# Grouping the value products of an attention stage, and the order of work around them

## The chip, the cores and the metric

The kernel runs on one core of one Trainium2 chip. TensorE (PE; its weight loads are listed apart as PEld) multiplies, VectorE (DVE), ScalarE (ACT) and GpSimd (POOL) work elementwise, SyncE (SP) issues most DMAs. Each engine takes its own queue in program order and waits on semaphores of the others. The metric is the device time of one execution in microseconds (us).

## The reference

```python
q_rot, k_rot = (rotate(q), rotate(k))            # 4 batches, 8 heads, 576 tokens, 64 per head
scores = scale * np.matmul(q_rot, k_rot.transpose(0, 1, 3, 2))
scores = scores - np.max(scores, axis=-1, keepdims=True)
attn = np.exp(scores)
attn = attn / (np.sum(attn, axis=-1, keepdims=True) + 1e-09)
x = np.matmul(attn, v)                           # to (2304, 512)
x = moe(x)                                       # RMS norm, gate and value (512 -> 1536), silu, out
return moe2(x)                                   # 8 experts, one per token
```

All three parts run in one launch. The change lies in the first, attention.

## The kernel before, in words

The 32 heads are taken as 16 pairs. The method `attention` is a loop over steps g; five steps are a head, ten a pair. `plan` is a table of actions with an offset each: an action of head i falls on step 5 i + offset, one of a pair p on step 10 p + offset, and within a step the actions are issued in the table's order, which is the order in every engine's queue. The actions that matter here:

- `ropeA`, `ropeC`, `ropeH`, `ropeL` rotate q and k of a pair (GpSimd's products, VectorE's sum, ScalarE's copy of the high part, VectorE's low part).
- `TQ` transposes a head's q and k with ten TensorE products into two PSUM tiles `t1` and `t2`; `TE` copies them out on ScalarE (first q, then k).
- `SM` makes the scores of one fifth of the queries (`s`), whose maximum over the keys VectorE takes (L288); `MT` transposes the five maxima of a head (L296), and a DMA carries them into a row of `qB`.
- `ST` makes the scores with keys on partitions (`sT`, four products, L312 and L314), and ScalarE takes their exponential into `E` (L315). `s`, `sT` and `t1` share three PSUM buffers in turn (`psA`), so each waits until the third one before it has been emptied.
- `AV` (L327) multiplies `E` with the values `vraw`: half u of the queries is a sum over five blocks j of keys, for the two heads of the pair in the left and right 64 columns of the array. It issues one block, two products, per step. The last block has 64 keys; both heads' share one tile, in the upper and lower 64 rows. `UE` copies the result out on ScalarE, scaled and squared.
- `EP` (GpSimd) and `ED` (VectorE) add four blocks of `E`; `DN` makes from them the denominators and `SQ` the sums of squares, with 32-column tiles, into a PSUM tile of a single buffer (`psC`, shared with `t2` and the transposed maxima); `stat` adds them up on VectorE at once.
- After every fourth pair, `W0` and `W` take reciprocals and roots of these sums and scale the batch's rows on VectorE, in pieces that `wstep` issues, two a step. From g = 70 on, `conv_step` converts weights of the next part, one piece in ten steps, on step 9 of each (`gr=(9,)`).

Behind attention stand the gated part (up to some 850 us) and the experts; the change touches no line of theirs.

## Time and profile before

| | us |
|---|---|
| median of 3 runs | 1163.78 |
| lowest, highest | 1163.47, 1176.99 |
| span of the profiled execution | 1164.5 |
| TensorE busy | 1071.4 (92%) |
| VectorE busy | 746.5 (64%) |
| ScalarE busy | 462.8 (40%) |
| GpSimd busy | 351.3 (30%) |

The profile is of one execution; its span runs from the first to the last instruction. Busy times are sums over a span with stages of very different limits, so a change in attention has to be read from the rows of that stage. The ends of TensorE's products are modelled and overlap the next start; intervals between starts are what the engine really takes. A granted clock of 1.00 is TensorE's 2.4 GHz, 0.50 is 1.2 GHz.

### The profile page before, as it was taken

The page shows a single profiled execution, that of the slowest core. Times are in us where ns is not written, and L with a number is a line of the kernel's source. Part 1 is how long each engine was busy: PE and PEld are TensorE (multiplying, and loading weights), DVE is VectorE, ACT ScalarE, POOL GpSimd, SP SyncE. Part 2 cuts the span into 40 slices and gives each one's busy share as a digit, 9 for nine tenths or more (in the row PEclk, how much of TensorE's full clock was granted, in tenths as well). Part 3 has the DMA queues.
Part 4 walks back from the last instruction along what each step waited for, and adds up shares of the span by engine and source line. Part 5 has one row for each costly group of instructions (what it writes and reads, how often), then busy time and mean ns, then how long its engine had stood idle before and what let it go on. Part 6 is the DMA issues. An engine that isn't in the chain of part 4 may idle for free. (4 is left out here: it accounts for less than half of the span.)

```text
span 1164.5 us, 17859 instructions
## 1 busy us (share of the span) xinstructions
PE 1071.4 (92%) x6406; PEld 873.1 (75%) x6406; DVE 746.5 (64%) x1415; ACT 462.8 (40%) x992; POOL 351.3 (30%) x374
## 2 busy tenths in 40 slices
PE   4999999999998899999999999999998979999595
PEld 3756656655565589899999999998877858988383
DVE  7587878889875856556565555562477645654263
ACT  3555555555556432422222222222345434533152
POOL 7547657657725501112011110110011211311211
PEclk9889989999999999999999999999999999999798
DMA  4333353343231201111122111101065655653464
GB/s 128 77 78 88 82 139 101 95 113 106 75 92 42 86 19 47 55 40 55 34 97 68 46 37 46 46 10 55 29 229 163 207 162 174 217 181 118 141 217 120
DMA packets 75990, 113.97 MB, mean 98 GB/s; under 512 B 18537, under 2 KB 43393, under 8 KB 75843
## 3 DMA queue, kind: packets, MB, share of 16 engines
q1 hardware_dynamic: 72162, 100.25, 29.8%
q0 software_dynamic: 3680, 11.91, 3.0%
q8 instruction: 74, 1.21, 0.5%
q14 instruction: 74, 0.60, 0.2%
HBM read 85.91 MB, written 12.17 MB: 84 GB/s over the span
## 5 line engine op out<-in xcount | busy, mean ns | idle before, releaser
L733 PE MATMUL gv<-xh,whi 128*128 128x384 f32 x576 | 197.0, 342 | 0.9 <-ACT xh L711 0.9
L733 PE MATMUL gv<-xl,whi 128*128 128x384 f32 x576 | 194.7, 338 | 0.5 <-DVE xl L715 0.5
L733 PE MATMUL gv<-xh,wlo 128*128 128x384 f32 x576 | 194.6, 338 | 0.0
L315 ACT ACTIVATE E<-sT 128x576 f32<-128x576 f32 (+1 forms) x160 | 104.0, 650 | 142.8 <-PE sT L314 142.8
L288 DVE TENSOR_REDUCE m<-s 128x1 fp32r<-128x576 f32 (+1 forms) x160 | 119.1, 749 | 61.2 <-PE s L287 58.5
L647 POOL TENSOR_TENSOR wlo<-cvt,whi 128x256 fp32r<-128x256 f32 x66 | 50.9, 774 | 334.0 <-ACT whi L646 333.9
L743 DVE TENSOR_TENSOR s<-s,gv 128x384 f32<-128x384 f32 x72 | 39.7, 553 | 154.3 <-PE gv L733 147.0
L327 PE MATMUL av<-E,vraw 128*64 128x288 f32 (+1 forms) x640 | 116.5, 444 | 1.5 <-ACT sq L338 1.3
L733 PEld LDWEIGHTS gv<-xh,whi 128*128 128x128 f32 x576 | 108.9, 189 | 6.4 <-issue 3.4
L733 PEld LDWEIGHTS gv<-xl,whi 128*128 128x128 f32 x576 | 109.1, 189 | 2.3 <-DVE xl L715 0.8
L742 ACT ACTIVATE s<-gv 128x384 f32<-128x384 f32 x72 | 34.9, 492 | 187.3 <-PE gv L733 187.3
L733 PEld LDWEIGHTS gv<-xh,wlo 128*128 128x128 f32 x576 | 108.9, 189 | 0.0
L312 PEld LDWEIGHTS sT<-qT,kT 128*128 128x128 f32 (+1 forms) x320 | 47.2, 187 | 67.5 <-issue 31.9
L761 PE MATMUL yps<-whi,hh 128*128 128x512 f32 x216 | 87.6, 406 | 6.4 <-ACT yacc L766 5.4
L312 PE MATMUL sT<-qT,kT 128*128 128x288 f32 (+1 forms) x320 | 86.4, 353 | 5.4 <-DVE m L288 2.4
L776 DVE TENSOR_TENSOR yacc<-yacc,yps 128x512 f32<-128x512 f32 x99 | 67.8, 686 | 32.3 <-PE yps L761 30.9
L345 POOL TENSOR_TENSOR e<-E 128x576 f32<-128x576 f32 x32 | 48.5, 1517 | 126.3 <-DVE es L349 117.7
L761 PE MATMUL yps<-wlo,hh 128*128 128x512 f32 x216 | 85.6, 396 | 0.0
L761 PE MATMUL yps<-whi,hl 128*128 128x512 f32 x216 | 85.6, 396 | 0.0
L287 PE MATMUL s<-kT,qT 128*128 128x288 f32 (+1 forms) x320 | 78.5, 333 | 3.5 <-DVE m L288 2.4
L1266 POOL DMA_INDIRECT x<-ysc,ix x27 | 32.9, 1219 | 152.9 <-DVE vi L1103 76.5
L1373 POOL DMA_INDIRECT out<-cvt,ix x20 | 23.5, 1176 | 166.7 <-DVE cvt L1371 114.2
(285 smaller groups left out, 2131.9 us busy)
## 6 DMA issues: line engine op xcount, KB each, us to landing
raw<-in_w SPq DMA_DIRECT2D x52, 512.0 KB
stt<-in_w SPq DMA_DIRECT2D x26, 512.0 KB
stt<-in_w_gate SPq DMA_DIRECT2D x24, 256.0 KB
stt<-in_w_val SPq DMA_DIRECT2D x24, 256.0 KB
stt<-in_w_out SPq DMA_DIRECT2D x24, 256.0 KB
qB<-qT SPq DMA_DIRECT2D x32, 144.0 KB
kB<-kT SPq DMA_DIRECT2D x32, 144.0 KB
qT<-qT SPq DMA_DIRECT2D x32, 144.0 KB
```

What stands on the lines that cost most here:

```text
L287: nc.tensor.matmul(s[:n, u, 0:288], qA[:, j * 128:j * 128 + n], kA[:, u * 288:u * 288 + 288], start=True, stop=True)
L288: nc.vector.tensor_reduce(m[:n, j:j + 1], s[:n, :, 0:288], axis=AX.XY, op=ALU.max)
L312: nc.tensor.matmul(s[:n, u, 0:288], kA[:, j * 128:j * 128 + n], qA[:, u * 288:u * 288 + 288], start=True, stop=False)
L315: nc.scalar.activation(e.rearrange("p (u c) -> p u c", u=2), s[:n, :, 0:288], AF.Exp, scale=0.125)
L327: self.nc.tensor.matmul(av[64 * h:64 * h + 64, 0:288], V[r, x, j * 64:j * 64 + 64], E[r, x, j, 288 * u:288 * u + 288], start=(j == 0), sto ...
L345: self.nc.gpsimd.tensor_tensor(t, E[:, h, 2 * k, :], E[:, h, 2 * k + 1, :], op=ALU.add)
L647: nc.gpsimd.tensor_tensor(lo, f, fr(hi), op=ALU.subtract)
L733: nc.tensor.matmul(t[:, :CH], w[:, k], r[:, k], start=(n == 0), stop=(n == 11))
L742: nc.scalar.activation(s, ps[0][:, :CH], AF.Silu)
L743: nc.vector.tensor_tensor(s, s, ps[1][:, :CH], op=ALU.mult)
L761: nc.tensor.matmul(ps, l, r[:, 2], start=(n == 0), stop=(n == tot - 1))
L776: nc.vector.tensor_tensor(old[:, t], old[:, t], ps, op=ALU.add)
```

## The change

Value products: `AV` issues all five blocks of a half at one step (ten products), at steps 13 and 18 of a pair where blocks stood at steps 10 to 19; `DN` stays at 18 and `SQ` goes from 21 to 23, each behind a group. From step 160 on, in the tail, blocks are issued singly as before. The last block takes all 128 rows: the values of the two heads lie in tiles of their own whose other half is zeros. `TQ` transposes 128 rows in the fifth block, too. `ED` goes from step 11 to 8, the rotations of q and k are issued apart, the low parts and rotations of VectorE go to other steps (`early` keeps the first two pairs), `stat` is issued at the end of the next step, `wstep` issues four pieces on the step of a value group and one on three others, and the conversion goes from step 9 to step 3.

```diff
     plan = (
-        ("UE1", 20), ("UE0", 15), ("ST", 0), ("MT", -3), ("TQ", -10), ("SM", -8), ("AV", 10), ("TEq", -10), ("LV", 3),
-        ("SQ", 21), ("ropeHq", -14), ("ropeHk", -14), ("QD", -4), ("TEk", -10), ("ropeLq", -13), ("DN", 18),
-        ("EP0", 5), ("ropeA", -21), ("ropeLk", -13), ("ED", 11), ("LQ", -13), ("ropeCk", -15), ("ropeCq", -16),
-        ("EP1", 5),
+        ("UE1", 20), ("UE0", 15), ("ST", 0), ("MT", -3), ("TQ", -10), ("SM", -8), ("AV", 13), ("TEq", -10), ("LV", 3),
+        ("SQ", 23), ("ropeHq", -14), ("ropeHk", -14), ("QD", -4), ("TEk", -10), ("ropeLq", -13), ("DN", 18),
+        ("ropeAq", -21), ("EP0", 5), ("EP1", 5), ("ropeAk", -20), ("ropeLk", -12), ("ED", 8), ("LQ", -13), ("ropeCk", -15),
+        ("ropeCq", -17),
     )
+    early = {"ropeLk": -13, "ropeCq": -16, "ropeAk": -21}
...
         for i in range(2):
-            self.raw["v", i] = sm.tile([P, 2, 320], F32, name=f"vraw{i}")
+            t = self.raw["v", i] = sm.tile([P, 2, 320], F32, name=f"vraw{i}")
+            nc.gpsimd.memset(t[64:128, 0, 256:320], 0.0)
+            nc.gpsimd.memset(t[0:64, 1, 256:320], 0.0)
...
-                    self.nc.sync.dma_start(t[64 * h:64 * h + 64, 0, 256:320], s2[h, 512:576, :])
+                    self.nc.sync.dma_start(t[64 * h:64 * h + 64, h, 256:320], s2[h, 512:576, :])
...
-            for j in range(4):
-                nc.tensor.transpose(t1[:, x, j * 128:j * 128 + 128], src[:, h * 5 + j].rearrange("p e d -> p (e d)"), self.idr)
-            nc.tensor.transpose(t2[:, x * 64:x * 64 + 64], src[:64, h * 5 + 4].rearrange("p e d -> p (e d)"), self.idr[:64, :64])
+            for j in range(5):
+                o = t1[:, x, j * 128:j * 128 + 128] if j < 4 else t2[:, x * 128:x * 128 + 128]
+                nc.tensor.transpose(o, src[:, h * 5 + j].rearrange("p e d -> p (e d)"), self.idr)
...
         for h in range(2):
-            r, x = (slice(0, n), h) if j < 4 else (slice(64 * h, 64 * h + 64), 0)
-            self.nc.tensor.matmul(av[64 * h:64 * h + 64, 0:288], V[r, x, j * 64:j * 64 + 64],
-                                  E[r, x, j, 288 * u:288 * u + 288], start=(j == 0), stop=(j == 4))
+            self.nc.tensor.matmul(av[64 * h:64 * h + 64, 0:288], V[:, h, j * 64:j * 64 + 64],
+                                  E[:, h if j < 4 else 0, j, 288 * u:288 * u + 288], start=(j == 0), stop=(j == 4))
...
-        self.stat(b, hp, 0, d)
+        self.later.append((b, hp, 0, d))
...
-        self.stat(b, hp, 1, d)
+        self.later.append((b, hp, 1, d))
...
             elif nm == "AV":
-                p, y = divmod(g - off, 10)
-                ok(self.AV, p, y // 5, y % 5)
+                if g >= 10 * NPAIR:
+                    if g < 10 * NPAIR + 10:
+                        self.AV(NPAIR - 1, *divmod(g - 10 * NPAIR, 5))
+                elif (g - off) % 5 == 0:
+                    p, y = divmod((g - off) // 5, 2)
+                    for j in range(5):
+                        ok(self.AV, p, y, j)
...
         for g in range(-25, 10 * NPAIR + 16):
+            late_stats, self.later = self.later, []
             for nm, off in self.plan:
                 act(nm, off)
+            if g >= 10 * NPAIR:
+                late_stats, self.later = late_stats + self.later, []
+            for x in late_stats:
+                self.stat(*x)
...
             elif g % 5 != 0:
-                wstep(2)
+                wstep(4 if g % 5 == 3 else 1)
...
-T = dict(wz=0, pi=8, ck="g", ck8="", c1=0, g0=70, gm=10, gr=(9,), w4=3, p0=8, u0=-1, ...
+T = dict(wz=0, pi=8, ck="g", ck8="", c1=0, g0=70, gm=10, gr=(3,), w4=3, p0=8, u0=-1, ...
```

TensorE's queue in the fourth pair before, from a transpose of the maxima (`t3`, step 2 of the ten) through three steps:

```order
L296 MATMUL t3_1072<-idr_65,m1_124 8x128
L287 MATMUL s_1077<-kT_1038,qT_1033 128x288 x2
L327 MATMUL av_1030<-E_748,vraw0_114 64x288 x2
L312 MATMUL sT_1083<-qT_774,kT_779 128x288 x2
L314 MATMUL sT_1083<-qB_777,kB0_116 128x288 x2
L287 MATMUL s_1089<-kT_1038,qT_1033 128x288 x2
L327 MATMUL av_1030<-E_748,vraw0_114 64x288 x2
L312 MATMUL sT_1098<-qT_774,kT_779 64x288 x2
L314 MATMUL sT_1098<-qB_777,kB0_116 64x288 x2
L287 MATMUL s_1104<-kT_1038,qT_1033 128x288 x2
L327 MATMUL av_1030<-E_748,vraw0_114 64x288 x2
```

And now, from the transpose of the same maxima on, to the start of the head behind them:

```order
L302 MATMUL t3_1065<-idr_65,m1_128 8x128
L293 MATMUL s_1070<-kT_1033,qT_1028 128x288 x2
L318 MATMUL sT_1074<-qT_769,kT_774 128x288 x2
L320 MATMUL sT_1074<-qB_772,kB0_120 128x288 x2
L293 MATMUL s_1080<-kT_1033,qT_1028 128x288 x2
L332 MATMUL av_1084<-E_746,vraw0_114 64x288 x10
L375 MATMUL d_1098<-sq_875,selh_124 32x144 x4
L318 MATMUL sT_1105<-qT_769,kT_774 64x288 x2
L320 MATMUL sT_1105<-qB_772,kB0_120 64x288 x2
L293 MATMUL s_1111<-kT_1033,qT_1028 128x288 x2
```

Where each step had a value product, one step of five now has ten with the square sums (`d`) behind, and four have none.

The transposes of a head (`t1`, `t2`) in the same queue, before:

```order
L260 MATMUL t1_1120<-idr_65,qhl_923 128x128 x4
L261 MATMUL t2_1121<-idr_65,qhl_923 128x64
L260 MATMUL t1_1120<-idr_65,khl_925 128x128 x4
L261 MATMUL t2_1121<-idr_65,khl_925 128x64
L287 MATMUL s_1132<-kT_1038,qT_1033 128x288 x2
L327 MATMUL av_1136<-E_748,vraw0_114 64x288 x2
```

and now:

```order
L267 MATMUL t1_1125<-idr_65,qhl_923 128x128 x4
L267 MATMUL t2_1126<-idr_65,qhl_923 128x128
L267 MATMUL t1_1125<-idr_65,khl_925 128x128 x4
L267 MATMUL t2_1126<-idr_65,khl_925 128x128
L293 MATMUL s_1137<-kT_1033,qT_1028 128x288 x2
L318 MATMUL sT_1155<-qT_899,kT_904 128x288 x2
```

All ten have one shape, and no value product follows the maxima's product.

VectorE's queue in the sixth pair, from the copy of the transposed maxima (`mr`, step 7) on, before; `qhl` and `khl` are low parts, `y`, `y2` the root's steps, `m1` the maxima:

```order
L298 COPY mr_1685<-t3_1683 8x128
L288 TENSOR_REDUCE m1_124<-s_1688 128x1
L243 TENSOR_TENSOR qhl_1669<-A_1474,qhl_1669 128x10x64
L243 TENSOR_TENSOR khl_1671<-A_1476,khl_1671 128x10x64
L457 TENSOR_TENSOR y2_1592<-y_1591 128x144
L459 TENSOR_TENSOR y2_1592<-y2_1592,ms_1589 128x144
L288 TENSOR_REDUCE m1_124<-s_1708 128x1
```

and now:

```order
L304 COPY mr_1679<-t3_1677 8x128
L294 TENSOR_REDUCE m1_128<-s_1682 128x1
L249 TENSOR_TENSOR qhl_1660<-A_1478,qhl_1660 128x10x64
L452 TENSOR_SCALAR y_1669<-ms_1667 128x144
L294 TENSOR_REDUCE m1_128<-s_1698 128x1
L249 TENSOR_TENSOR khl_1662<-A_1527,khl_1662 128x10x64
L354 TENSOR_TENSOR es_1641<-es_1641,e2_1643 128x576
L454 TENSOR_SCALAR y_1669<-y_1669 128x144
L456 TENSOR_TENSOR y2_1670<-y_1669 128x144
L458 SCALAR_TENSOR_TENSOR y2_1670<-y2_1670,ms_1667 128x144
L460 SCALAR_TENSOR_TENSOR y_1669<-y2_1670,y_1669 128x144
L294 TENSOR_REDUCE m1_128<-s_1738 128x1
```

The low part of k, the sum of exponentials and four root steps now stand behind one maximum, that of step 8, where TensorE has its ten value products.

## Rows read from the trace of the kernel before

**Rows 1.** Windows: us, busy us (count) by engine, TensorE's clock, DMA share, GB/s.

```profile
core 0 of [0], span 1164.5 us
...
91.60:112.03 20.43, 20.38 (x154) 13.18 (x155) 14.79 (x21) 11.84 (x26) 13.63 (x15) 1.00 0.36 88
132.50:333.00 200.50, 189.85 (x1393) 121.42 (x1393) 172.20 (x262) 109.93 (x240) 126.78 (x127) 0.97 0.38 99
333.00:369.50 36.50, 35.24 (x269) 21.70 (x267) 23.59 (x42) 18.80 (x41) 15.02 (x10) 1.00 0.32 86
```

**Rows 2.** Timeline, TensorE, one step: start, us, product, count.

```profile
98.31 0.53 PE L312 MATMUL sT<-qT,kT 128*128 128x288 f32 x2
98.68 0.43 PE L314 MATMUL sT<-qB,kB 65*128 65x288 f32 x2
98.95 0.43 PE L287 MATMUL s<-kT,qT 128*128 128x288 f32 x2
99.31 0.71 PE L327 MATMUL av<-E,vraw 128*64 128x288 f32 x4
99.94 0.48 PE L312 MATMUL sT<-qT,kT 128*64 128x288 f32 x2
```

**Rows 3.** Timeline, TensorE, a maxima product before the first value product.

```profile
39.80 0.48 PE L287 MATMUL s<-kT,qT 128*128 128x288 f32 x2
40.12 0.42 PE L312 MATMUL sT<-qT,kT 128*128 128x288 f32 x2
```

**Rows 4.** Timeline, TensorE, the denominator's products.

```profile
109.47 0.70 PE L362 MATMUL d<-es,sel 128*32 128x144 f32 x16
109.98 0.43 PE L362 MATMUL d<-E,selh 128*32 128x144 f32 x8
110.34 0.47 PE L312 MATMUL sT<-qT,kT 128*64 128x288 f32 x2
```

**Rows 5.** Timeline, TensorE, the transposes of a head.

```profile
102.15 0.46 PE L260 MATMUL t<-idr,qhl 128*128 128x128 f32 x4
102.53 0.25 PE L261 MATMUL t<-idr,qhl 64*128 64x64 f32 x1
102.71 0.53 PE L260 MATMUL t<-idr,khl 128*128 128x128 f32 x4
...
103.35 0.54 PE L287 MATMUL s<-kT,qT 128*128 128x288 f32 x2
```

**Rows 6.** Timeline, VectorE: a rotation before the first value product, a maximum.

```profile
35.06 2.10 DVE L231 TENSOR_TENSOR A<-A,B 128x640 f32<-128x640 f32 x1
...
99.42 0.76 DVE L288 TENSOR_REDUCE m<-s 128x1 fp32r<-128x576 f32 x1 [0.41 <-PE s L287]
```

**Rows 7.** Timeline, ScalarE, around the transposes of a head.

```profile
101.66 0.50 ACT L335 ACTIVATE x<-av,gcol 128x288 f32<-128x288 f32 x1 [0.29 <-PE av L327]
102.35 0.65 ACT L315 ACTIVATE E<-sT 128x576 f32<-128x576 f32 x1
103.28 0.58 ACT L269 CAST qT<-t 128x512 fp32r<-128x512 f32 x1 [0.28 <-PE t L260]
103.87 0.60 ACT L269 CAST kT<-t 128x512 fp32r<-128x512 f32 x1
```

**Rows 8.** Groups by line, 91.6 to 333.0: count, busy us, mean ns, idle before.

```profile
L243 DVE TENSOR_TENSOR khl<-A,khl 128x640 fp32r<-128x640 f32 x11 | 20.5, 1860 | 0.0
L349 DVE TENSOR_TENSOR es<-es,e 128x576 f32<-128x576 f32 x22 | 19.7, 897 | 0.0
L231 DVE TENSOR_TENSOR A<-A,B 128x640 f32<-128x640 f32 x22 | 17.9, 815 | 0.0
L238 ACT CAST qhl<-A 128x640 fp32r<-128x640 f32 x11 | 7.9, 717 | 0.0
```

**Rows 9.** Windows, the last stretch without value products and the one behind it.

```profile
33.80:40.60 6.80, 5.24 (x37) 4.45 (x36) 6.04 (x8) 5.04 (x10) 5.23 (x6) 1.00 0.30 67
40.60:50.80 10.20, 9.95 (x40) 6.67 (x38) 5.07 (x8) 3.90 (x8) 5.36 (x6) 0.50 0.35 87
```

More of the change, by code (lines that the diff above doesn't have):

```diff
@@ L193, in dm, with ropeA @@
         self.nc.sync.dma_start(fr(o), fr(i))
-    def ropeA(self, p):
-        for nm in "qk":
+    def ropeA(self, p, x):
+        if p == 0 and x == "k":
+            return
+        V, G = self.nc.vector, self.nc.gpsimd
+        for nm in x if p else "qk":
             for n in "AB":
                 self.st[n, nm, p] = self.rp.tile([P, 2, 320], F32, tag=n, name=n, bufs=3 if n == "A" else 2)
-        V, G = self.nc.vector, self.nc.gpsimd
         if p > 0:
-            for nm in "qk":
-                self.rope_cos(G, p, nm)
-                self.rope_sin(G, p, nm, (0, 1))
+            self.rope_cos(G, p, x)
+            self.rope_sin(G, p, x, (0, 1))
             return
@@ L269, in TE @@
         nc.scalar.copy(dst[:, 0:512], fr(t1[:, x]))
-        nc.scalar.copy(dst[:, 512:576], fr(t2[:, x * 64:x * 64 + 64]))
+        nc.scalar.copy(dst[:, 512:576], fr(t2[:, x * 128:x * 128 + 64]))
         st[nm + "A", i] = dst
@@ L320, in AV @@
     def AV(self, p, u, j):
-        n, E, V = PJ[j], self.st["E", p], self.raw["v", p % 2]
+        E, V = self.st["E", p], self.raw["v", p % 2]
         if j == 0:
@@ L511, in attention @@
         wait = [0]
+        self.later = []
         def wstep(n):
@@ L525, in at, with roped @@
             return q if r == 0 else -1
+        def roped(nm, off):
+            q = max((g - off) // 10, 0)
+            for i in (q - 1, q, q + 1):
+                o = self.early.get(nm, off) if i < 2 else off
+                if i >= 0 and g == 10 * i + o + self.lag.get((nm[4], i), 0):
+                    return i
+            return -1
         def lagged(nm, off, per):
@@ L558, in act @@
                 ok(self.SQ, q)
+                q = late(off + 1, self.sqt)
                 if q >= 0 and q % 4 == 3:
@@ L573, in act @@
                     self.loads(p + 2, "qk")
-            elif nm[:4] == "rope" and len(nm) == 6:
-                ok(getattr(self, nm[:5]), lagged(nm[4], off, 10), nm[5])
-            elif nm == "ropeA":
-                ok(self.ropeA, at(g, off, 10))
+            elif nm[:4] == "rope":
+                ok(getattr(self, nm[:5]), roped(nm, off), nm[5])
             elif nm[:2] == "EP":
@@ L850 @@
 SIZES = (128, 256, 288, 352, 384)
-T = dict(wz=0, pi=8, ck="g", ck8="", c1=0, g0=70, gm=10, gr=(9,), w4=3, p0=8, u0=-1, pp=[(1, 1), (1, 3), (2, 1), (2, 3), (3, 1), (3, 3)], w3=4, sqt=12, edt=4, dnt=7, ck2="g", ws=2, ws2=4, u2=1, c2=1, wy=0, yt={0: 1, 2: 1, 3: 2, 4: 1}, yr={0: 2, 2: 2, 3: 1, 4: 1}, bt={1: (0, 1), 2: (2, 2), 3: (3, 3), 5: (4, 5)}, yl={0: 1, 2: 1, 3: 1, 4: 2}, ba={0: (1, 2), 2: (1,), 3: (1,), 4: (1, 3, 5)})
+T = dict(wz=0, pi=8, ck="g", ck8="", c1=0, g0=70, gm=10, gr=(3,), w4=3, p0=8, u0=-1, pp=[(1, 1), (1, 3), (2, 1), (2, 3), (3, 1), (3, 3)], w3=4, sqt=12, edt=4, dnt=7, ck2="g", ws=2, ws2=4, u2=1, c2=1, wy=0, yt={0: 1, 2: 1, 3: 2, 4: 1}, yr={0: 2, 2: 2, 3: 1, 4: 1}, bt={1: (0, 1), 2: (2, 2), 3: (3, 3), 5: (4, 5)}, yl={0: 1, 2: 1, 3: 1, 4: 2}, ba={0: (1, 2), 2: (1,), 3: (1,), 4: (1, 3, 5)})
 class Ring:
```

## The prediction

> **What bounds the kernel now.** I read the windows view first, to find the stage that the change touches. All of it lies in the attention stage, 16 pairs of heads of ten steps each, up to 369.5 us; the 795 us behind it run the same instructions in both programs and only move with the end of attention. In an undisturbed pair TensorE is busy for 20.38 of 20.43 us, VectorE for 14.79, ScalarE for 11.84, GpSimd for 13.63 [rows 1]: TensorE is the bound there, and the others have room. Nine further pairs (132.5 to 333.0) take 200.5 us, 16.5 more than nine times 20.45; the mean clock of 0.97 accounts for about 6.0 of it, so some 10.4 us come from VectorE being late, which does 172.2/9 = 19.1 us of work a pair there, since weights are converted and rows scaled besides [rows 1].
>
> Then the timeline of TensorE, for what it is busy with. Five starts in a row show one step: scores 0.37 + 0.27, the row maxima's products 0.36, a value product pair 0.63 [rows 2]. The same maxima product with no value product behind it takes 0.32 where the start behind a small transpose is in it [rows 3]; the second half of the scores, which stands next to no change of shape, takes 0.27 for two. So around a value product the neighbours lose 0.10 (scores) and 0.09 (maxima). What the value product itself needs is read from the denominator's products, which run several column tiles in a row: 16 records, four tiles at a time, take 0.51 us, 0.128 a pass of 144 columns; the last 8 take 0.36 with the edge behind them, so the edge is about 0.10 to 0.13 [rows 4]. 288 columns are then 0.25 a pass, and two passes 0.50. One value step costs 0.63 + 0.19 = 0.82, of which 0.32 are edges.
>
> **Part 1, ten value products in a row.** A pair had ten such insertions and gets two. Each saves 0.32: 8 x 0.32 = 2.6 us a pair of TensorE. A group costs 5 x 0.50 + 0.13 = 2.63, and 0.09 ahead of it. The denominator and square sums stood behind value products before and still do: nothing.
>
> **Part 2, 128 rows for the last 64 keys.** The transposes with 64 rows take 0.18 each against 0.38 for four full ones, 0.095 each [rows 5]. Ten full ones are 0.95 against 1.20 measured: 0.25 a head, 0.5 a pair. The value product of the last keys also takes all rows, half of them zeros; it streams the same 288 columns, nothing. Four new memsets at the start are hidden by GpSimd's wait for the first load (bounds: 0, and at most 1 us without that cover).
>
> Together TensorE needs 20.4 - 3.1 = 17.3 us a pair. The question is whether anything lets it.
>
> **Part 3, what stands in the steps without value products.** Before, each step gave TensorE 1.6 us, and VectorE (a maximum takes 0.75 [rows 6]) and ScalarE (an exponential takes 0.65 [rows 7]) answered in its shadow. Now eight steps in ten take TensorE 0.54 + 0.27 = 0.81, and the waits for three score buffers and for the maxima's transpose (which waits for the fifth maximum) come within reach. So I walk one half pair along each queue, from one maxima transpose to the next, with a consumer starting 0.2 behind the slot of its product (98.95 + 0.27 + 0.2 is 99.42, where the maximum starts [rows 6]).
>
> The half with the denominator: 0.06 + 0.32 to the end of the first maxima product, 0.54 and 0.27 to 1.19, 0.09 + 2.63 to 3.91, denominator 0.87 [rows 4] to 4.78, scores 0.64 to 5.42. ScalarE had nothing to do from its last exponential until 5.62, and now everything comes at once: exponential 0.55 (ends overlap by 0.1), the value rows and their squares 0.69, the next exponential 0.55, copy of transposed q 0.59, of k 0.60 [rows 7]: 8.6. The copy of k holds the buffer of the last maxima product: 0.27, 0.2, maximum 0.75: the next transpose is at 9.9. The high parts of q and k (0.72 each [rows 8]) stand in ScalarE's queue ahead of an exponential that the value group waits for: 0.2 more, 10.1. The half with the square sums: 0.38 instead of 0.87 (two passes and an edge) gives 9.4 by ScalarE, but VectorE has a rotation of 0.82 [rows 8] between the last two maxima; with it, and GpSimd on the same tiles, I take 9.9 (bounds 9.6 and 10.4: the same rotation took 2.10 in the steps before the first value product [rows 6]). A pair is 20.0 us, not 17.3: it saves 0.45 of 20.45.
>
> Eleven pairs (the fourth to the fourteenth) at 0.45: -5.0. The late VectorE work, 10.4 us: the sums, rotations, low parts, conversion and four scaling steps are now queued in the step of the value group. From the maximum ahead of a group to the next one are 4.0 and 4.5 us in the walk; VectorE has 0.75 + 0.90 + 0.82 = 2.5 and 0.75 + 1.86 + 0.90 = 3.5 of its own in them [rows 8], which leaves 2.5 us a pair for the 172.2/9 - 14.8 = 4.3 of extra work; I take half, -5.2 (bounds 0 and -10.4). The last two pairs, 36.5 us [rows 1]: the very last has no maxima and no transposes, so it keeps its 2.6; the one before keeps 0.45 and its present lateness of 0.9, which I round to 1.2 together: -3.8. The first three pairs start at the low clock and keep their order of rotations: 0. The clock: between 33.8 and 40.6, the only stretch at full clock without value products, TensorE was busy for 5.24 of 6.80 us, waiting twice for VectorE and ScalarE, and the 10.2 us behind it ran at a granted 0.50 [rows 9], the 1.2 GHz level. I add half of the 6.0 lost now, +3.0 (bounds 0 and +33, below). The queues of SP: the scaling's stores and loads move by a few steps, with several steps of room: nothing.
>
> Sum: -5.0 - 5.2 - 3.8 + 3.0 = -11.0. The profiled execution has a span of 1164.5 us, 0.7 above the median of 1163.8; 1164.5 - 11.0 - 0.7 = 1152.8, so **1153 us**.
>
> The Trainium skill's page TensorEngine Tiling (Array Packing), section Performance Considerations, speaks against the change: tiling quickens TensorE but not the emptying of PSUM, which may become the bottleneck. Taken as a rule on busy time it would not bind, as 14.8 and 11.8 us of VectorE and ScalarE are under 17.3, and the sum would be that of the first rival; the rows above bind by order, not by busy time.
>
> **Rivals.** *One: the queues keep up, and TensorE's saving arrives.* For it: VectorE idles 0.41 us ahead of a maximum [rows 6], and by busy time no engine is in the way. Against: the chain of ScalarE above. Pairs without extra work fall to 17.3 (two pairs, -6.2), the nine to VectorE's 19.1 (-28), the last two to 17.3 + 12.6 (-6.6), the first three perhaps by 1 each: -44, 1120 us.
>
> *Two, slower: the clock.* If the bursts of short steps with waits bring the clock to 0.50 once in every pair, as after 40.6 [rows 9], where 10.2 us at half speed lost 5.1, and the value group lifts it after half that time, each of 13 pairs loses 2.6: +34, 1187 us. Against: TensorE is dense for 2.7 to 3.6 us in each half, and the nine pairs that wait for 10.7/9 = 1.2 us each kept a mean of 0.97 [rows 1]. It decides over 2% from 2.6 us a pair on. The Trainium skill's page TensorE: Matmul & The Clock Gate, section A second HAM failure mode: psum-queue depth-cycling, tells of a kernel in which short idle gaps between groups of products, while it cycles through PSUM buffers, made the clock swing between its levels; that is this case, and rows 9 are its one sight here.
>
> *Three: the change does not do what it says.* If two column tiles in a row still pay their edge at each product, as each does now at 0.63, a group takes 3.15 instead of 2.63: 0.52 in each of 30 halves, +15, 1168 us. Against: the denominator's passes follow at 0.128 with no edge between them [rows 4].
>
> **How the numbers follow.** Forecast (its own range 1142 to 1167, from the bounds of the two half walks and of the late work): 0.53. Rival one: 0.22, rival two: 0.12, rival three: 0.13. The range 1128 to 1182 leaves out half of rival one and two thirds of rival two, 0.19. What a measurement of this kernel can tell from no change is about 2%, 23 us: faster is below 1140.5 (rival one and the low edge of the forecast, 0.25), slower above 1187 (the upper half of rival two and what may add to rival three, 0.10), within it 0.65.
>
> **What would show it.** In the profile after: ten value products in about 2.6 us with no gap (more than 3.1 is rival three); ten transposes in under 1.0 us; undisturbed pairs of 20.0 us with TensorE busy for some 17.5 and 2 to 3 us of waits for ScalarE's copies of k and VectorE's maxima. Pairs near 17.3 would be rival one; granted clocks of 0.8 to 0.9 in most pairs rival two. The forecast fails first in the walk: if ScalarE can empty its queue earlier than I have it, each 0.5 us of a half is 13 us of the kernel.

## The result and the profile after

The changed kernel takes 1180.1 us (median of four runs, 1176.2 to 1181.6). Against the runs of the kernel before on the same chip its ratio is 1.0136, interval 1.0090 to 1.0181: slower by 1.4%, where 1153 us and a gain were forecast. The ratio is of fast runs alone: two of the four runs of the kernel before there, 1177.0 and 1178.1 us, were slow ones. Later runs of the kernel before, 13 to 19 beside each set of experiments, have medians of 1162.4 to 1164.5 us. The profiled execution has a span of 1179.1 us against 1164.5.

The windows view of the kernel after, in the same columns as [rows 1]: an undisturbed pair, the nine pairs with VectorE's extra work, and the last two.

```profile
core 0 of [0], span 1179.1 us
...
86.60:106.70 20.10, 18.39 (x157) 13.51 (x156) 12.72 (x20) 11.39 (x26) 13.01 (x15) 1.00 0.37 89
126.70:349.60 222.90, 181.53 (x1395) 137.97 (x1394) 178.18 (x264) 107.38 (x241) 125.68 (x126) 0.89 0.34 90
349.60:384.30 34.70, 31.65 (x272) 22.64 (x271) 21.54 (x38) 18.47 (x42) 12.32 (x10) 1.00 0.32 83
```

The balance by stage: the first three pairs are 5.0 us shorter (they end at 86.6 instead of 91.6), the two undisturbed pairs 0.8 (40.1 against 40.9), the nine pairs **22.4 longer** (222.9 against 200.5), the last two 1.8 shorter, and what lies behind attention is the same (794.8 against 795.0). The sum is +14.6. A part of this is work that changed windows: weights are converted in six units, of which five lay in the nine pairs before and one in the fifteenth, while now all six lie in the nine. Over ten pairs, the sixth to the fifteenth, the work is the same, and they take 242.9 us against 221.8, **21.1 longer**. So one stage took more than the whole difference, and the question is what happens there.

Two numbers of the row say what kind of time it is. TensorE stands idle there for 222.9 - 181.5 = 41.4 us, of which an undisturbed pair's 1.7 accounts for 15.3; 26.1 are new waits, against 10.2 before. And it is busy for 16.4 us more than nine undisturbed pairs (18.35 each), which I put down to the clock (0.89), against 6.2 before.

The waits of TensorE in the nine pairs, after (what waited, for whom, us in total, times, longest):

```profile
engine line waited for: us in total, times, longest us
PE t L267 <- DVE stat L386: 25.3, 7, 5.7
PE t L267 <- DVE stat L384: 7.5, 4, 5.1
PE t L302 <- DVE m L294: 3.1, 7, 0.5
PE s L293 <- ACT kT L275: 2.7, 9, 0.3
```

The transposes of q and k (L267) wait for `stat`, the addition of denominators and square sums, which has to empty the single buffer of `psC` first. The addition itself takes 0.29 us; the timeline of one such wait, VectorE, GpSimd and TensorE (start, duration, instruction, idle before and its releaser), shows what it stood behind:

```profile
start us, us, engine line op out<-in xcount [idle before <-releaser]
251.76 1.35 DVE L237 TENSOR_TENSOR A<-A,B 128x640 f32<-128x640 f32 x1
252.39 1.99 POOL L350 TENSOR_TENSOR es<-E 128x576 f32<-128x576 f32 x1
252.81 0.45 PE L375 MATMUL d<-sq,selh 128*32 128x144 f32 x8
253.04 1.52 DVE L468 SCALAR_TENSOR_TENSOR y<-y,y 128x144 f32<-128x144 f32 x1
...
254.35 1.47 POOL L350 TENSOR_TENSOR e<-E 128x576 f32<-128x576 f32 x1
...
254.59 1.40 DVE L487 SCALAR_TENSOR_TENSOR stat<-stat,y 128x144 f32<-128x144 f32 x1
...
254.67 0.53 PE L267 MATMUL t<-idr,qhl 128*128 128x128 f32 x4
...
255.79 1.59 POOL L225 TENSOR_TENSOR A<-qraw,cs 128x640 f32<-128x640 f32 x1
255.91 1.62 DVE L676 TENSOR_SCALAR ct<-ct 128x256 f32<-128x256 f32 x1
...
257.56 0.49 DVE L677 TENSOR_SCALAR ct<-ct 128x256 int32<-128x256 int32 x1
258.09 0.62 DVE L678 SCALAR_TENSOR_TENSOR ct<-stt,ct 128x256 int32<-128x256 int32 x1
258.75 0.62 DVE L679 SCALAR_TENSOR_TENSOR ct<-stt,ct 128x256 int32<-128x256 int32 x1
259.30 0.74 DVE L294 TENSOR_REDUCE m<-s 128x1 fp32r<-128x576 f32 x1
...
259.97 0.29 DVE L384 COPY stat<-d 128x144 f32<-128x144 f32 x1
...
260.31 0.37 PE L267 MATMUL t<-idr,qhl 128*128 128x128 f32 x1 [5.11 <-DVE stat L384]
```

The square sums' products end near 253.2, and their buffer is emptied at 260.3. Between them VectorE runs two pieces of the root (1.52 and 1.40), four conversion operations (3.35) and a maximum. TensorE does four transposes into `t1` and then stands for 5.11 us. The clock in the stretches ahead of this wait, in it, behind it and after that (windows, kernel after):

```profile
250.00:255.20 5.20, 5.20 (x45) 3.26 (x43) 5.17 (x7) 2.51 (x7) 4.11 (x3) 1.00 0.20 57
255.20:259.50 4.30, 0.00 (x1) 0.00 (x0) 4.20 (x6) 0.63 (x2) 4.30 (x6) 1.00 0.02 4
259.50:266.40 6.90, 6.09 (x27) 5.60 (x27) 4.44 (x8) 4.00 (x9) 0.25 (x1) 0.51 0.43 105
266.40:270.80 4.40, 4.40 (x52) 2.87 (x52) 2.34 (x4) 0.49 (x2) 1.12 (x1) 1.00 0.57 164
```

So TensorE comes out of the wait at 1.2 GHz and stays there for some 6 us before the grant is 1.00 again: at half the clock these cost some 3 us more (an estimate, half of the 6).

### The profile page after: what moved, and what is told of

Same layout as the page of the kernel before. It is cut to its first block, busy times and chain, and to the rows that moved or that the text cites. A ratio compares the mean times of both kernels' runs of the same rounds, so it can differ in the third digit from the quotient of the medians.

```text
span 1179.1 us, 17884 instructions
## 1 busy us (share of the span) xinstructions
PE 1045.3 (89%) x6406; PEld 888.0 (75%) x6406; DVE 745.1 (63%) x1415; ACT 457.0 (39%) x992; POOL 346.8 (29%) x378
## 5 line engine op out<-in xcount | busy, mean ns | idle before, releaser
L293 PE MATMUL s<-kT,qT 128*128 128x288 f32 (+1 forms) x320 | 84.2, 352 | 7.7 <-ACT kT L275 6.4
L332 PE MATMUL av<-E,vraw 128*64 128x288 f32 x640 | 88.2, 420 | 1.4 <-ACT sq L343 1.4
L318 PE MATMUL sT<-qT,kT 128*128 128x288 f32 (+1 forms) x320 | 78.7, 331 | 3.0 <-DMA qT<-qT 1.9
L350 POOL TENSOR_TENSOR es<-E 128x576 f32<-128x576 f32 x32 | 47.8, 1492 | 108.3 <-PE d L367 90.4
L320 PE MATMUL sT<-qB,kB 65*128 65x288 f32 (+1 forms) x320 | 75.3, 320 | 0.8 <-DMA qB<-mr 0.8
```

Source lines behind the costliest of these rows:

```text
L293: nc.tensor.matmul(s[:n, u, 0:288], qA[:, j * 128:j * 128 + n], kA[:, u * 288:u * 288 + 288], start=True, stop=True)
L318: nc.tensor.matmul(s[:n, u, 0:288], kA[:, j * 128:j * 128 + n], qA[:, u * 288:u * 288 + 288], start=True, stop=False)
L320: nc.tensor.matmul(s[:n, u, 0:288], kB[0:65, j * 128:j * 128 + n], qB[0:65, u * 288:u * 288 + 288], start=False, stop=True)
L332: self.nc.tensor.matmul(av[64 * h:64 * h + 64, 0:288], V[:, h, j * 64:j * 64 + 64], E[:, h if j < 4 else 0, j, 288 * u:288 * u + 288], sta ...
L350: self.nc.gpsimd.tensor_tensor(t, E[:, h, 2 * k, :], E[:, h, 2 * k + 1, :], op=ALU.add)
```

## Experiments

The first theory (A) was that the deferral of `stat` to the next step did it; its rival (B), that VectorE has too much work wherever the addition stands. Later theories are named in the expectations. Ratios are against runs of the kernel before beside them. "Clean" is the mean of the fourth and fifth pair, "nine" the sixth to fourteenth together, "ten" the sixth to fifteenth, "beyond" what the nine take above nine clean ones, "idle" and "clock" TensorE's idle time and granted clock in the nine; all are from the windows view. Only "ten" holds the same work in every row: where the conversion is issued at step 8 or 9 (before, e2, e4, e5, e8, e11, e16), its last unit falls into the fifteenth pair. Each row of windows is of one execution, and the runs of one kernel lie up to 13 us apart (e3: 1157.5 to 1170.0; e15: 1188.3 to 1201.2), so a difference of a few us between two rows is not settled by them. The expectations count pairs from 0: their pairs 8 to 13 are the ninth to the fourteenth.

| kernel | clean | nine | ten | beyond | idle | clock | ratio (interval) |
|---|---|---|---|---|---|---|---|
| before | 20.45 | 200.5 | 221.8 | 16.5 | 10.7 | 0.97 | 1 |
| the change | 20.05 | 222.9 | 242.9 | 42.5 | 41.4 | 0.89 | 1.0136 (1.0090 to 1.0181) |
| e11 128 rows alone | 19.55 | 195.8 | 216.7 | 19.9 | 14.5 | 0.98 | 0.9924 (0.9891 to 0.9957) |
| e4 group alone | 20.40 | 216.2 | 239.6 | 32.6 | 28.1 | 0.91 | 1.0149 (1.0095 to 1.0204) |
| e8 four pieces alone | 20.40 | 218.7 | 239.0 | 35.1 | 17.1 | 0.91 | 1.0121 (1.0068 to 1.0175) |
| e16 128 rows, deferral | 19.90 | 211.7 | 232.0 | 32.6 | 17.9 | 0.92 | 1.0043 (1.0017 to 1.0070) |
| e1 change, no deferral | 19.65 | 221.1 | 244.3 | 44.3 | 34.6 | 0.88 | 1.0226 (1.0153 to 1.0300) |
| e3 change, two pieces | 20.05 | 208.4 | 228.4 | 28.0 | 32.6 | 0.93 | 0.9984 (0.9953 to 1.0015) |
| e2 change, conversion at step 9 | 20.05 | 215.6 | 240.6 | 35.2 | 32.7 | 0.90 | 1.0176 (1.0122 to 1.0231) |
| e5 e3, conversion at step 8 | 20.05 | 207.0 | 233.6 | 26.6 | 31.3 | 0.93 | 1.0083 (1.0053 to 1.0113) |
| e7 change, no group | 19.90 | 261.8 | 288.2 | 82.7 | 48.0 | 0.82 | 1.0577 (1.0513 to 1.0641) |
| e15 e7, no deferral | 19.45 | 232.1 | 253.1 | 57.1 | 29.1 | 0.87 | 1.0242 (1.0174 to 1.0310) |
| e14 change, all dealt out | 20.10 | 203.5 | 223.3 | 22.6 | 26.2 | 0.94 | 1.0022 (0.9996 to 1.0047) |
| e13 128 rows, all dealt out | 19.55 | 186.8 | 206.3 | 10.9 | 7.7 | 1.00 | 0.9851 (0.9804 to 0.9899) |

### One part alone: e11, e4, e8

```diff
 e11, in the kernel before: TQ, TE, AV, loads and the value tiles as in the change; nothing else
 e4, in the kernel before:
-  ("AV", 10), ("SQ", 21)
+  ("AV", 13), ("SQ", 23)     and ten products at steps 13 and 18, as in the change
 e8, in the kernel before:
-                wstep(2)
+                wstep(4 if g % 5 == 3 else 1)
```

> The kernel before with only the last 64 keys on all 128 rows (five full transposes, zeroed halves of the value rows), products dealt out one to a step and VectorE's work as before. By the term of the prediction (0.25 us a head on TensorE, which has no idle time in a clean pair of the kernel before): clean pairs 19.9 us instead of 20.4, sixteen pairs 8 us less, total about 1156. Theory G (grouping is what shortens a clean pair of the change to 20.04): clean pairs stay near 20.4, total 1164. If TensorE's slack is what hides VectorE's work, the loaded pairs lose part of the gain: total 1158 to 1162.

> The kernel before with one part of the change alone: ten value products at a time at steps 13 and 18, square sums at step 23 behind a group; sums taken at once, conversion, scaling pieces, rotations and transposes as before. Theory A: undisturbed pairs fall from 20.45 to 20.0 to 20.3, and nothing stands ahead of stat, so loaded pairs stay at about 22: 1153 to 1162. Theory B: with TensorE quicker and VectorE's work the same, loaded pairs stay as they are too, but so do the rest: 1160 to 1166.

> The kernel before with only the pieces of scaling and root put as in the change: four on one step of five and one on the three others instead of two on four. Theory S (slack): the 0.8 us at every step hides part of the lump: pairs 8 to 13 longer by 0 to 1 us, total 1164 to 1170. Theory P (the four pieces make the wait whatever TensorE does): these pairs longer by 3 us each, total about 1180.

128 rows alone gain 0.8%, and an undisturbed pair gains 0.90 us, more than the prediction gave it. The timeline of TensorE in e11, a head's transposes between scores and maxima products, against [rows 5]:

```profile
84.84 0.55 PE L263 MATMUL t<-idr,qhl 128*128 128x128 f32 x5
85.23 0.59 PE L263 MATMUL t<-idr,khl 128*128 128x128 f32 x5
85.65 0.50 PE L289 MATMUL s<-kT,qT 128*128 128x288 f32 x2
```

They take 85.65 - 84.84 = 0.81 us where they took 1.20: 0.39 a head instead of 0.25. The group alone is slower by 1.5%; at 1179.8 us it lies beyond both theories. Its undisturbed pair is 20.40 us, as before: what TensorE no longer spends at edges (18.9 busy of 20.4) is all idle. And its nine pairs take 15.7 us more, though VectorE is busy for less in them than before (170.1 against 172.2 us); TensorE waits for maxima. The four pieces in a row alone cost 1.2%, in a kernel whose products are dealt out: the ninth to fourteenth pair take 3.0 us more each (151.2 against 133.2 together), as theory P had it. Of the 18.2 us more in the nine, 6.4 are idle time of TensorE and 11.8 busy time, at a lower granted clock (0.91 against 0.97). The nine pairs of e4 and of e8:

```profile
127.60:343.80 216.20, 188.07 (x1394) 133.59 (x1392) 170.13 (x260) 106.91 (x240) 130.22 (x126) 0.91 0.34 92
```

```profile
126.10:344.80 218.70, 201.63 (x1393) 127.67 (x1393) 174.46 (x262) 110.25 (x240) 126.06 (x127) 0.91 0.35 91
```

So two of the change's parts lose by themselves, and the one that gains is the one that touches neither order nor VectorE.

### The deferral: e1, e16

```diff
 e1, in the change: stat at the end of the step of its products
-            if g >= 10 * NPAIR:
-                late_stats, self.later = late_stats + self.later, []
+            late_stats, self.later = late_stats + self.later, []
 e16, e11 with:
-        self.stat(b, hp, 0, d)
+        self.later.append((b, hp, 0, d))     (likewise for SQ, which goes from 21 to 23)
```

> The changed kernel, but the sums (stat) are taken from their PSUM buffer at the end of the step that makes them, ahead of the scaling pieces and the conversion, instead of one step later behind them. Theory A (the single buffer): in the loaded pairs of the changed kernel TensorE waited 32.1 us at the transposes for stat, and the low clock behind these waits costs as much again as it lasts; with stat ahead of the extra work the waits at the transposes fall below 8 us between 189 and 350 us, the granted clock there rises from 0.86 to over 0.95, and the time is 1145 to 1158. Theory B (VectorE simply has too much work in these pairs): the wait moves to the next maximum, and the time stays within 6 us of the changed kernel, 1174 to 1186.

> e11_rows128_alone with the statistics added at the end of the next step (square sums two steps later, as in the change), VectorE's other work where it was before. If the deferral alone costs: clean pairs 19.9 instead of 19.55 and waits at stat of 2 us and more in pairs 8 to 13, total 1165 or more. If it costs only together with pieces in a row: clean pairs 19.6, total 1154 to 1160.

The waits of TensorE in the nine pairs of e1:

```profile
PE s L293 <- DVE m L294: 13.6, 7, 3.2
PE sT L318 <- DVE m L294: 12.5, 4, 4.0
PE t L302 <- DVE m L294: 2.3, 7, 0.7
```

Not one wait for `stat` is left, and the pairs are as long as in the change: now scores wait for the maximum that empties one of the three buffers of `psA`. Theory A falls as the cause of the loss; theory B had this move of the waits, and its range (1174 to 1186) is missed by 1 us (1187.1). The lump of VectorE's work stands ahead of whatever TensorE needs next, and the addition was only what happened to stand behind it. Yet the deferral is not free. An undisturbed pair gains 0.40 us without it (20.05 to 19.65), and with 128 rows alone it turns a gain of 0.8% into a loss of 0.4%, with waits for `stat` of up to 2.7 us:

```profile
PE t L263 <- DVE stat L382: 5.5, 3, 2.7
PE t L263 <- DVE stat L380: 3.4, 2, 1.7
```

Of the two things that e16 expected, it is the first, "the deferral alone costs", with one reserve: the square sums go to step 23 in it too.

### The size and place of VectorE's lumps in the change: e3, e2, e5

```diff
 e3, in the change:
-                wstep(4 if g % 5 == 3 else 1)
+                wstep(2)
 e2, in the change:              gr=(3,)  ->  gr=(9,)
 e5, in e3:                      gr=(3,)  ->  gr=(8,)
```

> The changed kernel with the scaling and root pieces issued two a step on four steps of five, as before the change, instead of four on the step of a value group. Theory A: only the waits behind four pieces go, a part of those at steps 0; conversions stay ahead of stat: 1168 to 1178. Theory B: no change beyond 6 us.

> The changed kernel with the weight conversion on step 9 of each pair, as before the change, instead of step 3. Theory A: the waits at the transposes behind the conversion (steps 5, about half of the 32 us) go, those behind the scaling pieces (steps 0) stay: 1158 to 1168. Theory B: VectorE has as much to do as ever: no change beyond 6 us, 1174 to 1186.

> The change, with two scaling or root pieces on each step (as e3_two_pieces), and with the four conversion operations at step 8 of a pair instead of step 3: there GpSimd stands idle (it waits for the denominators of the pair), while at step 3 it runs the rotation products that share the memory port with VectorE. Theory C (contention: the conversion holds VectorE too long because its operations take 0.77 to 1.11 us beside GpSimd): the four operations fall from 3.9 to about 2.5 us, the loaded pairs from 23.1 to 27.6 us to about 22 to 23, total near 1150. Theory L (a lump, of whatever length, ahead of a result that TensorE needs): operations shorter, but a wait of 2 us at the next result remains and the clock falls after it; pairs 23 to 26, total 1156 to 1163. Theory T (VectorE's total work in a loaded pair): no change, 1161.

Two pieces a step instead of four take 14.5 us out of the nine pairs, and as much out of the ten, and bring the kernel level with the one before: more than either theory had (1161.3 us, where A gave 1168 or more). The nine pairs of e3:

```profile
126.90:335.30 208.40, 175.80 (x1395) 131.68 (x1394) 172.96 (x264) 107.06 (x241) 126.18 (x126) 0.93 0.37 96
```

Moving the conversion to step 9, where it stood before, takes 7.3 out of the nine, but the fifteenth pair, which holds the last unit then, takes 25.0 instead of 20.0, so that 2.3 are left over ten and nothing in the time, 1183.2 us, as theory B had it. The waits scatter over maxima and `stat` (6.3, 6.2, 3.8 and 2.8 us): the place changes who is late, not that something is. At step 8 GpSimd was to be idle, but in the loaded pairs it is not. It waits for the denominators later there and runs beside the conversion, which took 4 x 0.76 = 3.0 us in the mean (0.67, 0.58, 0.89, 0.91) and in one pair 5.1; the nine pairs hardly differ from those of e3, and its total, 1173.9 us and above what all three theories gave, is worse, the pair behind them having taken 26.6 us. Theory C is neither shown nor excluded by this run, since the cover that it was to test was not there.

### Without the group: e7, e15

```diff
 e7, in the change:
-  ("AV", 13)     five blocks at steps 13 and 18
+  ("AV", 10)     one block a step, at 10 to 19, as before
 e15, e7 with stat in the same step, as e1
```

> The change with its value products dealt out one to a step again, two heads' at a time (first of a pair at step 10), as before; 128 rows, denominators and square sums behind, and the four pieces in a row all stay. Theory S (slack: the products dealt out give TensorE some 0.8 us of other work at every step, which hides VectorE's lumps; grouping takes it away): clean pairs 20.2 us, pairs 8 to 13 back to 22 to 24 us, total 1160 to 1168. Theory P (the four pieces in a row make the wait whatever TensorE does): pairs 8 to 13 stay at 24 to 30 us, total 1176 to 1184.

> e7_change_without_group with the statistics added at the end of the step of their products again, instead of the next. If the deferral is what makes that kernel slow (the one buffer is held a step longer, while four pieces or four conversion operations stand ahead of the addition): pairs 8 to 13 fall from 191.4 us in sum to 130 to 145, total 1164 to 1180, clean pairs 19.55 instead of 19.9. If the cause is the pieces in a row or the moved rotation work: 1200 or more.

Both theories of e7 missed: it is far slower than the change, 1229 us. Its clean pairs are shorter than those of the change and its loaded ones are the longest of all, with waits for `stat` of 31.1 and 15.8 us, one of 6.3, in the nine pairs. With the deferral undone (e15) 30 us come back, and again the waits pass to the maxima (16.3 and 10.1); at 1195.7 us, with 164.9 in the ninth to fourteenth pair, e15 lies between what its two theories gave. The change puts four pieces, and in every second half the conversion too, on just the steps of the value group (3 and 8 of a pair); there the group is 2.58 us of TensorE's work that hides a part. Take the group away and leave the lumps, and that part is bare. This is argued and not shown: how much of e7's excess falls to the rotations that the change moves as well was not tried apart.

### Dealt out: e6, e9, e10, e12, then e14 and e13

```diff
 the four conversion operations of a unit: one each on steps 3, 4, 8 and 9
-            V.tensor_scalar(f, f, ...)  ...  (four in a row)
+            self.cq += [four closures];   on those steps  self.cq.pop(0)()
 e6, e9 (in the change):                               wstep(2)
 e10, e14 (in the change):
-            elif g % 5 != 0:
-                wstep(4 if g % 5 == 3 else 1)
+            else:
+                wstep(1)
 e12, e13 (in e11):              gr=(9,)  ->  gr=(3,)
-            elif g % 5 != 0:
-                wstep(2)
+            else:
+                wstep(1)
```

In e6, e9, e10 and e12 the dealt out operations took the buffer of the unit behind theirs, so the first blocks' weights are other numbers, and the stages behind attention, where the data choose the visits, took other ways. (e9's expectation gives the early load as the reason; holding it back did not put this right.) Only their attention is read; e13 and e14 are e12 and e10 with the operations on their own buffers.

> The change, with two pieces on each step, and with the four conversion operations of a unit dealt out one to a step (steps 3, 4, 8 and 9) instead of all on step 3: the same work, no lump above 1 us. Theory L (lump): no wait above 1.5 us is left in pairs 8 to 13, the clock stays granted in full there, pairs at 20 to 21.5 us instead of 23.1 to 27.6; total about 1142 to 1148. Theory T (total work): the waits only divide, pairs stay above 23, total 1157 to 1163. Theory C (contention): the operations at steps 3 and 4 stay slow and those at 8 and 9 are fast, so about half of the gain of the run with the conversion at step 8.

> The change, two pieces on each step, the four conversion operations of a unit dealt out one to a step (3, 4, 8 and 9 of a pair), as in e6_conv_spread, but with the next unit's load held back until the last of the four is issued (in e6 the load went ahead of them, so that the weights of the first blocks there were wrong numbers and its later stages took other ways; only its attention is to be read). Theory L (lumps ahead of a result that TensorE needs): pairs 8 to 13 sum to about 134 us as in e6 (20.4, 20.6, 28.2, 23.4, 21.3, 20.5), against 160.0 in the change and 146 with two pieces alone; attention ends near 365, total 1153 to 1160. Theory T (VectorE's total work): 146 us or more in these pairs, total 1161 or more.

> As e9_conv_spread_in_order, and the scaling and root pieces dealt out too: one on every step (ten a pair) instead of two on four of five (eight a pair). Theory L: the waits of 3.4 us and 1.3 us that stayed in pair 10 (two root pieces of 1.4 to 1.5 us in one step) go or fall below 1.5 us, the clock stays granted in full there; pairs 8 to 13 sum to 124 to 129 us, attention ends at 355 to 361, total 1145 to 1155. Theory T: no gain over e9 or a loss, since more pieces come in a pair: 1156 or more.

> The kernel before with the last 64 keys on all 128 rows and with VectorE's conversion and pieces dealt out as in e10_all_dealt_out, value products dealt out one to a step as before. Theory S (products dealt out hide VectorE's work better than a group does): pairs 5 to 13 at 19.9 to 20.8 us, total 1143 to 1150, at most that of e10. Theory G (the group's 1.8 us of TensorE a pair are worth something once VectorE's work is dealt out): e10 is shorter than this by 0.3 us a pair or more.

> As e10_all_dealt_out, its operations on their own buffers: the change (products ten at a time, statistics deferred) with conversion and pieces dealt out. Theory G (the group's idle 1.8 us a pair are worth something once VectorE's work is dealt out): pairs 5 to 13 as short as those of e13 (186) or shorter. Theory S (products dealt out hide VectorE's work, the group bares it): as in e10, 201 to 207 us with one wait of 2.8 us and two of 1.7 at stat, attention end 366 to 371, total 1160 to 1168.

> As e12_rows128_all_dealt_out, in which (as in e6, e9 and e10) the dealt out operations worked on the next unit's buffer, so that the first blocks' weights were other numbers and the later stages took other ways; here on their own. The kernel before, with 128 rows, the conversion one operation to a step and one scaling or root piece on every step; value products dealt out one to a step. Theory L (lumps): pairs 5 to 13 as in e12 (19.4 to 21.9 us, sum 186 against 200.5 before), no wait above 1.1 us, attention ends near 344 instead of 369.5; with the stages behind as before, total 1139 to 1147. If VectorE's dealt out work comes back as a wait at the start of the next stage: 1148 to 1154.

The nine pairs: e6 196.3, e9 198.7, e10 207.4, e12 186.1 us. With the fifteenth they take 221.4, 222.8, 227.2 and 205.6. Dealing out the conversion alone takes the ten pairs from 228.4 (e3) to 221 to 223, less than the nine show, since the fifteenth pair waits for `stat` again (25.1 and 24.1 us against 20.0). So the same work in smaller portions is shorter here, as theory L wanted and theory T did not, but by less than L wanted: in e6 one wait of 3.4 us is left, and pairs of 28.1 and 23.4. Nor is a gain of 6 to 7 us between single executions clear of their scatter. Dealing out the pieces as well, one on every step, brings no further gain in the kernel with the group, where theory L expected one: the ten pairs take 227.2 (e10) and 223.3 (e14), and e14's time is level with that of the kernel before, as e3's is. For e14 theory S had the numbers right (203.5 us in the nine, 1164.7 in all). Windows of the nine pairs, e14 and e13:

```profile
126.40:329.90 203.50, 177.30 (x1394) 128.78 (x1394) 168.31 (x261) 106.31 (x241) 125.00 (x126) 0.94 0.36 97
```

```profile
124.10:310.90 186.80, 179.14 (x1392) 116.25 (x1392) 171.94 (x263) 111.05 (x240) 133.60 (x129) 1.00 0.41 107
```

Two kernels with the same pieces dealt out in the same way: with products dealt out too (e13) the nine pairs take 186.8 us, TensorE is idle for 7.7 of them and its clock is granted in full; in the change (e14) they take 203.5, with 26.2 idle. The two differ in the group, the deferral and the moved rotations and sums together, so the 16.7 us (17.0 over ten pairs) are the price of all of these, not of the group alone. VectorE does more in e13 (171.9 against 168.3 us) and is late less often. The waits of e13 in these pairs:

```profile
PE sT L314 <- DVE m L290: 3.1, 5, 1.7
PE t L263 <- DVE ms L477: 1.4, 2, 1.0
PE s L289 <- DVE m L290: 1.3, 3, 0.7
```

e13 takes 1147.4 us, ratio 0.9851 (0.9804 to 0.9899): 1.5% faster than the kernel before and 2.8% below the change. About half is from the 128 rows (e11), half from the dealing, by the middle values: the intervals of e11 and e13 just overlap. Its expectation was missed narrowly (at most 1147 us, no wait above 1.1; one of 1.7 is left).

## Why the prediction was wrong

**Right: the undisturbed pair.** The half-pair walks gave 10.1 + 9.9 = 20.0 us, measured 20.05. The group took 2.58 us (below) where 2.63 was worked out, so rival three, edges inside the group, is out; and the waits in such a pair are for the copy of k and the maxima, as the walk had them. TensorE is busy for 18.35 us and idle for 1.7 of it, where some 17.5 and 2 to 3 were forecast; a modelled end ahead of a wait counts as busy, so the two can't be told apart finely. The timeline of TensorE, kernel after: a group and what follows it, then the waits between groups.

```profile
112.55 2.65 PE L332 MATMUL av<-E,vraw 128*64 128x288 f32 x20
115.13 0.45 PE L375 MATMUL d<-sq,selh 128*32 128x144 f32 x8
```

```profile
99.44 0.49 PE L293 MATMUL s<-kT,qT 128*64 128x288 f32 x2 [0.34 <-ACT kT L275]
...
101.00 0.22 PE L302 MATMUL t<-idr,m 128*8 128x128 f32 x1 [0.55 <-DVE m L294]
```

But the source of the gain was put wrong. The prediction let grouping bring TensorE to 17.3 us and the waits take most of it back. The runs show that grouping gave the pair next to nothing (20.45 to 20.40 in e4; 19.45 without it and 19.65 with it in e15 and e1) and that the 128 rows gave 0.90 (19.55 in e11; 0.78 of it in the transposes), undersized there as 0.25 a head. The change keeps only 0.40 of that 0.90; e1 returns another 0.40 by undoing the deferral, for which the walk has no term. So that the pair came out at 20.0 is in part luck.

**The step that failed** is the term for the late VectorE work: "which leaves 2.5 us a pair for the 172.2/9 - 14.8 = 4.3 of extra work; I take half, -5.2 (bounds 0 and -10.4)". Measured, waits in the nine pairs rose from 10.2 to 26.1 us above the clean pairs' own: +15.9, outside both bounds. Two things were wrong in it.

First, it compared sums over a pair where the limit is one step. The cover of 2.5 us was counted against the mean extra work of a pair; but the change puts the extra work into one step, and there it is 6.3 us in the row shown (1.52 + 1.40 + 3.35) ahead of the next result that TensorE needs. That the portions are a cause, and not the amount, is shown by e3, in which the same pieces in smaller portions take 14.5 us out of the nine pairs and the whole loss out of the time, and by e8, in which the large portions alone, moved into the kernel before, cost 18.2. That the group takes cover away is shown by e4: with the portions of before and no more VectorE work, the nine pairs take 15.7 us more, in waits for maxima and at a clock of 0.91. The bound of zero rested on this too: it allowed the work to stay as late as before, not to delay a result that had been on time.

Second, it took VectorE's durations as fixed. Groups of the nine pairs by line and form (count, busy us, mean ns), before and after:

```profile
L488 DVE TENSOR_TENSOR x<-x,wb 128x384 f32<-128x384 f32 x8 | 6.2, 779 | 0.0
L655 DVE SCALAR_TENSOR_TENSOR ct<-stt,ct 128x256 int32<-128x256 int32 x5 | 3.0, 591 | 0.2
```

```profile
L493 DVE TENSOR_TENSOR x<-x,wb 128x384 f32<-128x384 f32 x8 | 8.0, 1000 | 0.0
L678 DVE SCALAR_TENSOR_TENSOR ct<-stt,ct 128x256 int32<-128x256 int32 x6 | 6.7, 1114 | 0.2
L249 DVE TENSOR_TENSOR khl<-A,khl 128x640 fp32r<-128x640 f32 x9 | 7.3, 814 | 0.0
```

At the places they were moved to, a scaling of 384 columns takes 1.00 us instead of 0.78 and the third conversion operation 1.11 instead of 0.59, while the low part of k falls to 0.81 from the 1.86 of [rows 8]. In an undisturbed pair VectorE is busy for 12.7 us where it was for 14.8 [rows 1]; the extra work of a loaded pair goes from 4.3 to 178.2/9 - 12.7 = 7.1, or, over ten pairs with the same six conversions, from 186.4/10 - 14.8 = 3.8 to 191.6/10 - 12.7 = 6.4. The change moved the slow places from the work of every pair, where it did not matter, to the extra work, where it did.

**The clock** was put at +3.0 (bounds 0 and +33) and came to +10.2. The mechanism of rival two was the right one, with another trigger: not the bursts of short steps in every pair (clean pairs keep 1.00 in every kernel here) but the long waits in the loaded ones. Of rival two's sum of +34 us, seven of the nine pairs with one or two dips each (ten in all, against two before) gave a third.

**Other terms.** The last two pairs gave 1.8 of the 3.8: the fifteenth, from which the conversion moved away, 1.3, and the last one 0.5 where 2.6 was put; why was not looked into. The first three gave 5.0 where 0 was put; that is not a firm saving, since e8, with the order of before there, is 6.3 us shorter in the same stretch. That VectorE's other work is "now queued in the step of the value group" was right, but the prediction did not ask what stands in front of what in VectorE's queue. Still open is the share of the moved rotations, which no run took apart, and why the costs do not add: the deferral costs 1.2% with 128 rows alone (e11 to e16) and 3.3% in the change without the group (e15 to e7), but nothing that these runs can show in the change itself (e1 against it, overlapping intervals).

## What to carry to other kernels

Compare an engine's extra work with the slack of the one step in which it is queued, ahead of the next result that the bound engine needs, and not with the slack of a whole period: the same pieces two a step on four steps, instead of four on one step and one on three, were worth 14.5 us of 242.9 here (the change to e3, ten pairs). Work of the bound engine that looks wasteful, such as products dealt out with an edge at each, can be the slack that hides another engine; price its removal by what it was hiding. And try the parts of a change alone: here one part gained 0.8%, two lost over 1% each, and the sum hid all three. Last, choose the stretch that is compared so that it holds the same work in both kernels.

## What the runs showed of the hardware

**VectorE instructions that ended just behind a GpSimd instruction beside them.** The timeline of VectorE and of GpSimd in the kernel before:

```profile
236.58 0.29 DVE L453 SCALAR_TENSOR_TENSOR y<-y,ms 128x144 f32<-128x144 f32 x1
236.91 1.47 DVE L455 SCALAR_TENSOR_TENSOR y<-y,y 128x144 f32<-128x144 f32 x1
```

```profile
236.80 1.41 POOL L345 TENSOR_TENSOR e<-E 128x576 f32<-128x576 f32 x1 [6.48 <-DVE es L349]
```

Two instructions of one kind and size take 0.29 and 1.47 us. The second starts 0.11 after GpSimd's has begun and ends 0.17 after GpSimd's end (238.38 and 238.21). In the lump shown above L468, L487 and L676 end 0.18, 0.17 and 0.15 us after the ends of L350, L350 and L225 in the same way; the maxima and `stat`, which read PSUM, stay at 0.75 and 0.29 throughout. The Trainium skill, page SBUF — State Buffer, section Who interferes with whom, says that "A DVE instruction with two SBUF inputs contends with a GpSimd instruction that reads SBUF", and calls their shared ports an exclusive lock. The rows of L455, L468 and L487, which have two inputs in SBUF, agree; L676 has one, so that sentence does not speak of it.

**The granted clock fell with each of ten long waits in the middle of dense work.** In the kernel after, in the pairs from the fourth on, there are ten waits of 1.5 to 5.7 us: in six the grant fell to 0.50 (1.2 GHz) within 2.1 us after the wait, in four while it still lasted, and it stayed there for 3 to 7 us. It is not so in every case: in e11 a wait of 1.96 us and in e13 one of 1.73 were followed by none, while two waits of 1.7 in e16 were.

**The transposes of 64 rows** cost 0.39 us a head more than full ones in their place (e11), though they do less.
